# Two channel transforms back to back in the second matrix product of a spectral mixer, with TensorE's order written by hand

## The chip, the cores and the metric

The kernel runs on one core of a Trainium2 chip. The core has a matmul engine (TensorE, PE in the profile), a vector engine (VectorE, DVE), an engine for activations (ScalarE, ACT), GpSimd (POOL) and SyncE (SP), which here only issues DMA. Each engine works through its own queue in order; semaphores make one engine wait for another. PSUM is the memory that matmuls write, in eight banks; SBUF holds everything else.

The metric is the device time of one execution in microseconds. Three runs of the kernel before took 389.78, 391.57 and 392.61 us; their median, 391.57 us, is the time to compare with.

## What is computed

The input x has 2048 tokens (S) and 512 channels (D), in float32. It is normalised over the channels; one branch filters the result in the frequency domain, the other normalises it once more and runs an MLP across the tokens. The two are multiplied and added to x:

```
xn = layernorm(x)
s  = irfft2(rfft2(xn) * (w_r + 1j * w_i))     # over tokens and channels, 2048 x 257 weights
h  = layernorm(xn)
u  = gelu(w1^T h + b1)                                       # over the token axis: 2048 -> 1792
g  = silu(w2^T u + b2)                                       # 1792 -> 2048
y  = x + s * g
```

## The kernel before, in words

The 2048 output rows lie in 16 row blocks of 128. The program has three stages. In the first, each block of x is normalised, the first step of its Fourier transform is taken on TensorE, and part of the product with w1 (GEMM1) is accumulated. In the second, the filter is applied to the spectrum while the rest of GEMM1 runs. The third stage, GEMM2, is the one that the change touches; it takes from about 212 us to the end.

**GEMM2's products.** The row blocks are taken in eight pairs: pair p holds block j0 = p and block j1 = p + 8. A pair is computed by seven half-size products in the manner of Strassen (with Winograd's additions). Each has 21 matmuls (L828): seven blocks of the hidden dimension (the list FORMS) times three, because every float32 operand is split into a high and a low part and three of the four partial products are kept. The seven products of a pair run in the order `ORDER = (1, 2, 5, 6, 3, 7, 4)`. On the hidden side the split operands are made once, and lie in the tiles fd, fa, fb and fc. On the side of w2 they are made for each product: `w2_forms` (L714) loads, adds (L720, L726) and splits, the high part by a copy on ScalarE (L706), the low part by a subtraction on VectorE (L707). The tile w2f has three buffers, so the form of one product is written when the product three places earlier is done.

**PSUM tiles.** Product 1 goes to the tile bx, 2 to by, 5 to bz. Products 6, 7 and 4 are added onto bx and product 3 onto bz. Between two products that share a tile, something must read it: `copied` (L790, ScalarE) takes p1 from bx after product 1, p5 from bz after product 5 and v2 from bx after product 6; `summed` (L798, VectorE) makes c11 after product 2, c12 after product 3, and c22 = bx + p5 after product 7. `gate` (L794, ScalarE) applies the silu, and `finish` (L802, VectorE) multiplies the gate by the spectral result in PSUM bank 0 or 1 and issues the accumulating store.

**The spectral branch inside GEMM2.** For each row block, `gathered` (L756, ScalarE) copies the block's spectrum out of ey into a tile yt. `channels` (L759 to L783) takes the inverse transform over the channels: four matmuls against ci (L763, shown as eight rows in the profile) into PSUM bank 6 (blocks j0) or 7 (blocks j1); od (L765, ScalarE); es (L767, L768), tt (L770, L771) and y (L776 to L779) on VectorE; and the split of y into ch (ScalarE) and cl (VectorE, both L143). The tiles od, es, tt and y have one buffer each. `spectral` (L785) then makes the inverse transform over the tokens with three matmuls of 512 columns (L146 to L148), which need ch and cl, into bank 0 or 1.

In the kernel before, the loop calls `channels` for block j1 behind product 6 and uses it behind product 7. It calls `channels` for the next pair's block j0 behind product 7, and uses it behind product 1 of the next pair.

**What sets the order.** The kernel is written in a layer that schedules: each engine's queue is laid down at build time by a scheduler that takes the instructions by the order of the program and by their readiness. Where a call goes through `keep` (tc.keep_in_program_order), the engine's order is that of the program. The class `Kept` (L124) wraps an engine so that every operation does. TensorE is wrapped so in the second stage; for GEMM2 the line `V, A, T = nc.vector, nc.scalar, nc.tensor` (L685) takes the wrapping off again.

Of the kernel before, what the change touches and what calls it, by code (L numbers as in the profile page):

```python
# [134 lines left out]
def spectral_mixer_kernel(tc, x, w1, b1, w2, b2, wk, we, wx, c_f, c_ft, c_d, c_i, c_g, c_h, out):  # L135
    nc = tc.nc
    V, A, G, T, SY = nc.vector, nc.scalar, nc.gpsimd, nc.tensor, nc.sync
# [4 lines left out]
    def split(hi, lo, src):  # L142
        return A.activation(hi, src, AF.Copy), V.tensor_sub(lo, src, hi.bitcast(F32))  # L143

    def mm3(o, lh, ll, rh, rl, first, last):
        T.matmul(o, lh, rh, start=first, stop=False)  # L146
        T.matmul(o, lh, rl, start=False, stop=False)  # L147
        T.matmul(o, ll, rh, start=False, stop=last)  # L148

    with tc.tile_pool(name="ps", bufs=1, space=PSUM) as psp, ExitStack() as left, ExitStack() as right:  # L150
# [38 lines left out]
        keep = tc.keep_in_program_order  # L189
# [143 lines left out]
        def form_parts(n, i):  # L333
            t, k = form[i][n]
            return t[:, k, :D // 2], t[:, k, D // 2:]
# [155 lines left out]
        T = Kept(T, keep)  # L491
# [193 lines left out]
        V, A, T = nc.vector, nc.scalar, nc.tensor  # L685
        w2p = pool(right, "right", "w2", 3)
        NP, HD = NJ // 2, D // 2
# [66 lines left out]
        def gathered(j):  # L754
            yt = fp.tile([P, 4, P], F32, name=f"yt{j}", tag="yt", bufs=2)
            A.activation(yt.rearrange("p b (l c) -> p b l c", c=2), ey[:, :, :, j], AF.Copy)  # L756
            return yt

        def channels(j, yt):  # L759

            pe = ps[:, 6 + j // NP].rearrange("p (h b c) -> p h b c", b=2, c=P)
            for b in range(4):
                T.matmul(pe[:, b % 2, b // 2], yt[:, b], ci[:, b], start=True, stop=True)  # L763
            od = fp.tile([P, 2, P], F32, name=f"od{j}", tag="od")
            A.activation(od, pe[:, 1], AF.Copy)  # L765
            es = fp.tile([P, 2, 2, P], F32, name=f"es{j}", tag="es")
            V.tensor_add(es[:, 0], pe[:, 0], od)  # L767
            V.tensor_sub(es[:, 1], pe[:, 0], od)  # L768
            t = fp.tile([P, 2, 64], F32, name=f"tt{j}", tag="tt")
            V.tensor_add(t[:, 0], es[:, 1, 1, :64], es[:, 1, 1, 64:])  # L770
            V.tensor_sub(t[:, 1], es[:, 1, 1, 64:], es[:, 1, 1, :64])  # L771
            y = fp.tile([P, D], F32, name=f"y{j}", tag="y")
            yv = y.rearrange("p (s h q c) -> p s h q c", s=2, h=2, c=64)
            ev = es[:, :, 0].rearrange("p h (q c) -> p h q c", c=64)
            ov = es[:, 0, 1].rearrange("p (h c) -> p h c", c=64)
            V.tensor_add(yv[:, 0, :, 0], ev[:, :, 0], ov)  # L776
            V.tensor_sub(yv[:, 1, :, 0], ev[:, :, 0], ov)
            V.scalar_tensor_tensor(yv[:, 0, :, 1], t, RT, ev[:, :, 1], op0=ALU.mult, op1=ALU.add)
            V.scalar_tensor_tensor(yv[:, 1, :, 1], t, -RT, ev[:, :, 1], op0=ALU.mult, op1=ALU.add)  # L779
            ch = fp.tile([P, D], F32R, name=f"ch{j}", tag="ch", bufs=2)  # L780
            cl = fp.tile([P, D], F32R, name=f"cl{j}", tag="cl", bufs=2)
            split(ch, cl, y)
            return ch, cl  # L783

        def spectral(j, y):  # L785
            mm3(ps[:, j // NP], cft[:, 0], cft[:, 1], *y, True, True)

        def copied(name, src):
            t = fp.tile([P, HD], F32, name=name, tag=name.split("_")[0])
            A.activation(t, src, AF.Copy)  # L790
            return t

        def gate(g, j, cols, src, scale):
            A.activation(g[:, cols], src, AF.Silu, bias=b2t[:, j:j + 1], scale=scale)  # L794

        def summed(name, a, b):
            t = fp.tile([P, HD], F32, name=name, tag="c", bufs=2)
            V.tensor_add(t, a, b)  # L798
            return t

        def finish(g, j, cols):
            V.tensor_mul(g[:, cols], ps[:, j // NP, cols], g[:, cols])  # L802
            if j + 1 < NJ:
                G.dma_start(out[:, j, cols], g[:, cols], accum_op=ALU.add)  # L804
            else:
                V.tensor_add(g[:, cols], g[:, cols], xr[:, cols])
                SY.dma_start(out[:, j, cols], g[:, cols])

        left_, right_, whole = slice(0, HD), slice(HD, D), slice(0, D)
        y0 = channels(0, gathered(0))  # L810
        for p in range(NP):
            j0, j1 = p, p + NP
            g0, g1 = (fp.tile([P, D], F32, name=f"g{j}", tag="g", bufs=2) for j in (j0, j1))
            bx, by, bz = ps[:, 2 + p % 2, :HD], ps[:, 4, :HD], ps[:, 5, :HD]
            for k, n in enumerate(ORDER):
                wf = ready.pop(0)
                w = next(wforms, None)
                if w is not None:
                    ready.append(w)
                if k == 1:  # L820
                    yt = gathered(j1)
                if k == 4 and p + 1 < NP:
                    yt = gathered(j0 + 1)
                o = {1: bx, 6: bx, 7: bx, 4: bx, 2: by, 5: bz, 3: bz}[n]
                for m, i in enumerate(FORMS):
                    uh, ul = form_parts(n, i)
                    for a, (wi, ui) in enumerate(((0, uh), (0, ul), (1, uh))):
                        T.matmul(o, wf[:, wi, i], ui, start=m + a == 0 and n in (1, 2, 5), stop=m == NH - 1 and a == 2,  # L828
                                 skip_group_check=n in (6, 3, 7, 4))
                if n == 1:  # L830
                    p1 = copied(f"p1_{p}", bx)
                    spectral(j0, y0)
                elif n == 5:
                    p5 = copied(f"p5_{p}", bz)
                elif n == 2:
                    gate(g0, j0, left_, summed(f"c11_{p}", by, p1), 1.0)
                elif n == 6:
                    v2 = copied(f"v2_{p}", bx)
                    y1 = channels(j1, yt)
                elif n == 3:  # L840
                    gate(g0, j0, right_, summed(f"c12_{p}", bz, v2), 1.0)
                    finish(g0, j0, whole)
                elif n == 7:
                    gate(g1, j1, right_, summed(f"c22_{p}", bx, p5), -1.0)
                    spectral(j1, y1)
                    if p + 1 < NP:
                        y0 = channels(j0 + 1, yt)
                    else:
                        finish(g1, j1, right_)
                else:  # L850
                    gate(g1, j1, left_, bx, -1.0)
                    finish(g1, j1, whole if p + 1 < NP else left_)
# [37 lines left out]
```

## Time and profile before

| What | us |
|---|---|
| median of three runs | 391.57 |
| the profiled execution's own time | 387.47 |
| span of the profile (first to last instruction) | 385.7 |
| mean granted TensorE clock in the profile | 0.993 of full speed |
| TensorE busy with matmuls | 374.0 (97% of the span) |
| VectorE busy | 323.2 (84%) |
| ScalarE busy | 227.6 (59%) |
| GpSimd busy | 78.6 (20%) |

The profile is one execution. The span is what the profile covers, and the execution's own time holds the little that lies around it. In the rows of a timeline the first figure is the start in us from the beginning of the span, the second the length in us; then come the engine, the line of the kernel, the operation, what it writes and reads, the shapes and how many instructions were merged in the row. A bracket gives the idle time of the engine ahead of the row, and what ended it. Rows of a windows view give a stretch, its length, the busy time of TensorE (and of more engines, where asked for) with counts, the granted clock, the share of the DMA engines and GB/s. Matmuls are pipelined and their ends are modelled, so that the distance from one start to the next says more than a row's length.

### The profile page before, as it was taken

Reading aid. Unit: us, or ns where it says so; the run is one execution under the profiler, and the core shown is the slowest. Engines: PE = TensorE matmul, PEld = TensorE weight load, DVE = VectorE, ACT = ScalarE, POOL = GpSimd, SP = SyncE. Lnnn points to the kernel's source line nnn. Section 1 sums busy time; section 2 is a strip of 40 time slices with the busy share of each in tenths; the row PEclk is TensorE's granted clock in tenths of the full one; section 3 lists DMA queues with packets and bytes.
Section 4 is the critical chain, followed back from the end, with each engine's and each line's share of the span. In section 5 each row is a group of like instructions: output and inputs, shape, how many; then the busy total and the mean of one; then the engine's idle time right before and its main releaser. Section 6 shows DMA issues by size and latency. Waiting matters only on the chain.

```text
span 385.7 us, 7939 instructions
## 1 busy us (share of the span) xinstructions
PE 374.0 (97%) x2872; PEld 328.8 (85%) x2872; DVE 323.2 (84%) x734; ACT 227.6 (59%) x412; POOL 78.6 (20%) x133
## 2 busy tenths in 40 slices
PE   7999999999999999999799989999999999999994
PEld 4888888888778878777588979999999999999994
DVE  5899999986579999897995999796979787887873
ACT  4677776764843455575417695565656564646541
POOL 2133233231302333233001003030202020210100
PEclk9999999999999999999899999999999999999999
DMA  8974777312636889988828398896979787885602
GB/s 262 300 251 155 266 254 241 97 55 82 198 77 173 211 226 256 245 226 193 259 71 253 57 274 208 214 215 166 201 153 214 140 230 143 220 165 156 98 0 55
DMA packets 39143, 70.01 MB, mean 182 GB/s; under 512 B 5424, under 2 KB 21440, under 8 KB 38976
## 3 DMA queue, kind: packets, MB, share of 16 engines
q1 hardware_dynamic: 30048, 48.14, 39.8%
q0 software_dynamic: 9056, 21.38, 29.3%
q8 instruction: 22, 0.36, 0.4%
q14 instruction: 17, 0.14, 0.1%
HBM read 61.10 MB, written 8.13 MB: 179 GB/s over the span
## 4 chain that ended last, share of the span: by engine, by line
PE 73%; DVE 9%; DMA 9%; issue 5%; ACT 1%; POOL 1%; SPq 0%; DVEq 0%; POOLq 0%; ACTq 0%
PE ps L828 28%; PE ps L377 20%; PE ps L132 16%; PE ps L241 4%; PE ps L763 3%; DMA s<-in_w_dram 2%; DMA out_dram<-g 2%; DVE w2f L707 2%; DMA w1l<-in_w_dram 2%; PE ps L366 1%; DMA w1s<-in_w_dram 1%; PE ps L147 1%; PE ps L148 1%; DMA hf<-in_c_h_dram 1%; DVE xc L589 1%
## 5 line engine op out<-in xcount | busy, mean ns | idle before, releaser
L377 PE MATMUL ps<-h,w1h 128*128 128x512 f32 x224 | 58.7, 398 | 0.0
L132 PE MATMUL ps<-h,w1h 128*128 128x512 f32 x152 | 49.6, 408 | 0.0
L707 DVE TENSOR_TENSOR w2f<-s,w2f 128x896 fp32r<-128x896 f32 x32 | 34.8, 1092 | 16.6 <-ACT w2f L706 15.8
L377 PEld LDWEIGHTS ps<-h,w1h 128*128 128x128 f32 x224 | 40.9, 188 | 7.9
L828 PE MATMUL ps<-fa,w2f 128*128 128x256 f32 x336 | 43.4, 282 | 0.0
L828 PE MATMUL ps<-fc,w2f 128*128 128x256 f32 x336 | 41.7, 280 | 1.0 <-DVE w2f L707 0.6
L828 PE MATMUL ps<-fb,w2f 128*128 128x256 f32 x336 | 42.5, 281 | 0.1
L828 PEld LDWEIGHTS ps<-fa,w2f 128*128 128x128 f32 x336 | 41.6, 188 | 0.8
L828 PEld LDWEIGHTS ps<-fc,w2f 128*128 128x128 f32 x336 | 40.3, 188 | 1.6 <-DVE w2f L707 0.8
L828 PEld LDWEIGHTS ps<-fb,w2f 128*128 128x128 f32 x336 | 40.4, 188 | 0.5 <-DVE c L798 0.5
L697 POOL DMA_DIRECT2D s<-in_w_dram x16 | 13.9, 870 | 122.0 <-DMA s<-in_w_dram 36.7
L706 ACT ACTIVATE w2f<-s 128x896 fp32r<-128x896 f32 x32 | 30.2, 949 | 14.1 <-DVE s L720 10.9
L132 PEld LDWEIGHTS ps<-h,w1h 128*128 128x128 f32 x152 | 27.7, 192 | 9.9 <-issue 4.9
L707 DVE TENSOR_TENSOR w2f<-a,w2f 128x896 fp32r<-128x896 f32 x24 | 26.0, 1085 | 9.5 <-ACT w2f L706 9.5
L132 PE MATMUL ps<-h,w1l 128*128 128x512 f32 x76 | 30.1, 396 | 2.8 <-DMA w1l<-in_w_dram 2.8
L377 PE MATMUL ps<-h,w1l 128*128 128x512 f32 x112 | 30.6, 389 | 0.0
L706 ACT ACTIVATE w2f<-a 128x896 fp32r<-128x896 f32 x24 | 22.8, 950 | 11.8 <-PE ps L828 7.3
L377 PEld LDWEIGHTS ps<-h,w1l 128*128 128x128 f32 x112 | 21.0, 188 | 4.5
L589 DVE SCALAR_TENSOR_TENSOR xc<-xc,turn,px 128x512 f32<-128x512 f32 x32 | 23.9, 747 | 0.2 <-issue 0.2
L372 DVE TENSOR_TENSOR w1l<-w1r,w1h 128x512 fp32r<-128x512 f32 (+1 forms) x32 | 20.9, 652 | 2.1 <-ACT w1h L369 1.9
L804 POOL DMA_DIRECT2D out_dram<-g x15 | 13.5, 902 | 43.8 <-DVE g L802 43.8
L794 ACT ACTIVATE g<-c,b2t 128x256 f32<-128x256 f32 x24 | 12.1, 505 | 15.9 <-DVE c L798 13.3
(128 smaller groups left out, 765.5 us busy)
## 6 DMA issues: line engine op xcount, KB each, us to landing
a<-in_w_dram SPq DMA_DIRECT2D x24, 448.0 KB, 4.0
wt<-in_wk_dram POOLq DMA_DIRECT2D x16, 512.0 KB, 4.7
s<-in_w_dram SPq DMA_DIRECT2D x16, 448.0 KB, 4.3
s<-in_w_dram POOLq DMA_DIRECT2D x16, 448.0 KB, 6.7
w1s<-in_w_dram SPq DMA_DIRECT2D x36, 128.0 KB, 3.2
w1r<-in_w_dram SPq DMA_DIRECT2D x16, 256.0 KB, 3.6
xc<-px SPq DMA_DIRECT2D x64, 64.0 KB, 4.1
x<-in_x_dram SPq DMA_DIRECT2D x15, 256.0 KB, 3.7
```

The costliest lines, as they stand in the source:

```text
L132: return lambda *args, **kw: self.keep(operation(*args, **kw))
L241: T.matmul(z[:, b], h[:, b * P:(b + 1) * P], c, start=True, stop=True)
L372: keep(V.tensor_sub(dst, src, hi.bitcast(F32)))
L377: T.matmul(ps[:, bank + i], w[wi][:, i * P:(i + 1) * P], hj, start=first and j == 0, stop=last and j == NJ - 1)
L589: V.scalar_tensor_tensor(to, zt, turn[:, k:k + 1], px[:, ::-1], op0=ALU.mult, op1=ALU.add)
L697: G.dma_start(t, w2_half(*added), accum_op=ALU.add)
L706: A.activation(wf[:, 0], v, AF.Copy)
L707: V.tensor_sub(wf[:, 1], v, wf[:, 0].bitcast(F32))
L763: T.matmul(pe[:, b % 2, b // 2], yt[:, b], ci[:, b], start=True, stop=True)
L794: A.activation(g[:, cols], src, AF.Silu, bias=b2t[:, j:j + 1], scale=scale)
L804: G.dma_start(out[:, j, cols], g[:, cols], accum_op=ALU.add)
L828: T.matmul(o, wf[:, wi, i], ui, start=m + a == 0 and n in (1, 2, 5), stop=m == NH - 1 and a == 2, skip_group_check=n in (6, 3, 7, 4))
```

## The change

Three things change in the loop over the pairs, and nothing else:

- both gathers of a pair stand early: block j1's at the second product, as before, and the next pair's block j0 at the third instead of the fifth;
- both calls of `channels` stand behind product 6, one behind the other; `spectral` stays where it was for either block;
- from the second pair on, T is the wrapped TensorE, so that its instructions (those of `channels` and `spectral` too, which use the same T) keep the program's order. In the first pair it is not wrapped.

```diff
--- before.py
+++ after.py
@@ -807,20 +807,20 @@
                 SY.dma_start(out[:, j, cols], g[:, cols])
 
         left_, right_, whole = slice(0, HD), slice(HD, D), slice(0, D)
-        y0 = channels(0, gathered(0))
+        y0 = [channels(0, gathered(0))]
         for p in range(NP):
             j0, j1 = p, p + NP
             g0, g1 = (fp.tile([P, D], F32, name=f"g{j}", tag="g", bufs=2) for j in (j0, j1))
             bx, by, bz = ps[:, 2 + p % 2, :HD], ps[:, 4, :HD], ps[:, 5, :HD]
+            yts = []
+            T = Kept(nc.tensor, keep) if p else nc.tensor
             for k, n in enumerate(ORDER):
                 wf = ready.pop(0)
                 w = next(wforms, None)
                 if w is not None:
                     ready.append(w)
-                if k == 1:
-                    yt = gathered(j1)
-                if k == 4 and p + 1 < NP:
-                    yt = gathered(j0 + 1)
+                if k in (1, 2) and (k == 1 or p + 1 < NP):
+                    yts.append(gathered((j1, j0 + 1)[k - 1]))
                 o = {1: bx, 6: bx, 7: bx, 4: bx, 2: by, 5: bz, 3: bz}[n]
                 for m, i in enumerate(FORMS):
                     uh, ul = form_parts(n, i)
@@ -829,23 +829,21 @@
                                  skip_group_check=n in (6, 3, 7, 4))
                 if n == 1:
                     p1 = copied(f"p1_{p}", bx)
-                    spectral(j0, y0)
+                    spectral(j0, *y0)
                 elif n == 5:
                     p5 = copied(f"p5_{p}", bz)
                 elif n == 2:
                     gate(g0, j0, left_, summed(f"c11_{p}", by, p1), 1.0)
                 elif n == 6:
                     v2 = copied(f"v2_{p}", bx)
-                    y1 = channels(j1, yt)
+                    y1, *y0 = (channels(j, yt) for j, yt in zip((j1, j0 + 1), yts))
                 elif n == 3:
                     gate(g0, j0, right_, summed(f"c12_{p}", bz, v2), 1.0)
                     finish(g0, j0, whole)
                 elif n == 7:
                     gate(g1, j1, right_, summed(f"c22_{p}", bx, p5), -1.0)
                     spectral(j1, y1)
-                    if p + 1 < NP:
-                        y0 = channels(j0 + 1, yt)
-                    else:
+                    if p + 1 == NP:
                         finish(g1, j1, right_)
                 else:
                     gate(g1, j1, left_, bx, -1.0)
```

## The prediction

> **What bounds the kernel now.** The page first, then TensorE's timeline over one pair of row blocks of GEMM2, and the windows row for the same stretch.
>
> ```profile
> span 385.7 us, 7939 instructions
> PE 374.0 (97%) x2872; PEld 328.8 (85%) x2872; DVE 323.2 (84%) x734; ACT 227.6 (59%) x412; POOL 78.6 (20%) x133
> ```
> ```profile
> 278.17 2.54 PE L828 MATMUL ps<-fd,w2f 128*128 128x256 f32 x21
> ...
> 288.67 1.05 PE L763 MATMUL ps<-cd,yt 128*128 128x128 f32 x8
> 289.48 2.72 PE L828 MATMUL ps<-fa,w2f 128*128 128x256 f32 x21
> 292.04 2.63 PE L828 MATMUL ps<-fb,w2f 128*128 128x256 f32 x21
> 294.51 0.39 PE L146 MATMUL ps<-ch,cft 128*128 128x512 f32 x1
> 294.74 0.38 PE L763 MATMUL ps<-cd,yt 128*128 128x128 f32 x2
> ...
> 295.64 0.83 PE L763 MATMUL ps<-cd,yt 128*128 128x128 f32 x6
> 296.23 2.72 PE L828 MATMUL ps<-fb,w2f 128*128 128x256 f32 x21
> 298.79 1.46 PE L828 MATMUL ps<-fd,w2f 128*128 128x256 f32 x11
> ```
> ```profile
> 277.00:299.00 22.00, 22.00 (x183) 21.60 (x183) 18.19 (x39) 12.20 (x22) 3.47 (x4) 1.00 0.84 185
> ```
>
> The timeline shows pair p=3. A pair runs seven products of 21 matmuls in the order 1, 2, 5, 6, 3, 7, 4. Product 1 starts at 278.17, the channel transform of the upper block (8 rows of L763) at 288.67 after product 6, product 3 at 289.48, product 7 at 292.04, the spectral triple (L146 to L148) with the second transform threaded into it at 294.51, product 4 at 296.23, and the next pair at 298.79. The period is 298.79 - 278.17 = **20.62 us**, and the windows row says TensorE is busy in all 22.00 us, VectorE (the third figure) in 18.19. So TensorE sets the pace here with no gap to win, and VectorE has only some 3.8 us of slack in 22: TensorE will wait wherever a needed VectorE instruction stands late in its queue.
>
> The one to look at is c22 (L798), which reads the PSUM tile bx after product 7. Product 4 adds onto the same tile, so its first matmul must wait for c22; in the built program of both kernels it does. VectorE around that point of the same pair, and the ScalarE instructions that feed it:
>
> ```profile
> 291.13 0.42 DVE L767 TENSOR_TENSOR es<-ps,od 128x256 f32<-128x256 f32 x1
> 291.47 0.41 DVE L768 TENSOR_TENSOR es<-ps,od 128x256 f32<-128x256 f32 x1
> 291.92 0.22 DVE L770 TENSOR_TENSOR tt<-es 128x64 f32<-128x64 f32 x1
> ...
> 292.80 0.29 DVE L779 SCALAR_TENSOR_TENSOR y<-tt,es 128x128 f32<-128x128 f32 x1
> 293.00 0.42 DVE L798 TENSOR_TENSOR c<-ps,v 128x256 f32<-128x256 f32 x1
> 293.33 1.09 DVE L707 TENSOR_TENSOR w2f<-a,w2f 128x896 fp32r<-128x896 f32 x1
> 294.33 0.69 DVE L143 TENSOR_TENSOR cl<-y,ch 128x512 fp32r<-128x512 f32 x1
> 294.94 0.69 DVE L802 TENSOR_TENSOR g<-ps,g 128x512 f32<-128x512 f32 x1
> 295.54 0.42 DVE L798 TENSOR_TENSOR c<-ps,p 128x256 f32<-128x256 f32 x1
> ```
> ```profile
> 293.12 0.63 ACT L143 ACTIVATE ch<-y 128x512 fp32r<-128x512 f32 x1
> 293.66 0.49 ACT L794 ACTIVATE g<-c,b2t 128x256 f32<-128x256 f32 x1
> ```
>
> c22 ends at 295.54 + 0.42 = 295.96, and product 4 starts at 296.23: the wait is covered by 0.27 us, and only because the second transform lies in between. In the last pair there is no second transform, and the wait shows:
>
> ```profile
> 377.61 0.40 PE L148 MATMUL ps<-ch,cft 128*128 128x512 f32 x1
> 378.10 2.74 PE L828 MATMUL ps<-fb,w2f 128*128 128x256 f32 x21
> ```
> ```profile
> 377.63 0.41 DVE L798 TENSOR_TENSOR c<-ps,p 128x256 f32<-128x256 f32 x1
> ```
>
> The spectral triple issues every 0.23 us (294.51 to 294.74), so product 4 could have started at 377.84; c22 ended at 378.04 and product 4 started at 378.10, 0.06 later. That is the price of one wake-up.
>
> **The change part by part.**
>
> *TensorE's work.* No instruction is added or removed. The second transform moves from the spectral triple to right behind the first. Both together take 2 x (289.48 - 288.67) = 1.62. Product 3 takes 292.04 - 289.48 = 2.56 behind a transform, product 7 294.51 - 292.04 = 2.47: switching back from a transform costs 0.09. From 288.67 product 4 can then start after 1.62 + 2.56 + 2.47 + 3 x 0.23 = 7.34, against 296.23 - 288.67 = 7.56 now. **Gain 0.22 us a pair**, at 296.01, if nothing waits.
>
> *VectorE's queue.* The diff moves `channels(j0 + 1, ...)` ahead of product 3, and the built program shows where its vector instructions land from p=1 on: es, tt, y of the upper block; es of the next block; cl of the upper block; tt and y of the next; c12; the L707 of the next pair's form 1; cl of the next; the g product L802; **only then c22**. In the kernel before, the next block's chain stood behind c22. What is newly in front, by start-to-start steps: es 2 x 0.34 (291.13 to 291.47) = 0.68; tt and y 293.00 - 291.92 = 1.08; cl 294.94 - 294.33 = 0.61; in all 2.37. One more wait: the upper block's ch ends at 293.12 + 0.63 = 293.75, while VectorE, done with the next es at 293.00 + 0.68, wants it at 293.68: 0.10 with the wake-up. c22 then runs from 295.54 + 2.47 = 298.01 to 298.43, and product 4 starts at 298.49. ScalarE doesn't add to it: c12 would start at 295.47 and end at 295.89, the next ch (0.63) and the gate (0.49) end by 296.7, and cl and L802 want them at 296.8 and 297.4.
>
> **The stall is 298.49 - 296.01 = 2.48 us a pair.** Queued behind the waiting matmul is all of TensorE: product 4, the next products 1, 2, 5, 6. Nothing gives it back. VectorE's chain starts anew from the end of product 6, through the ScalarE copy of form 4 into a buffer that product 6 frees, and so shifts along. New period 20.62 - 0.22 + 2.48 = **22.88**. I looked for a second wait: after c22 VectorE does form 2, then waits for the left gate, which waits for product 4 (301.0 + 0.49 for the gate), then L802, L707 of form 5, L720 (taken as L707's 1.09, same shape), a ScalarE copy, L707 of form 6, done near 307; product 6 starts at 309.1. Some 2 us spare, so none.
>
> *The order written by hand.* From p=1 on TensorE's built order differs between the two kernels only in the moved transform, so keeping it costs nothing by itself. Between the first pair and the second it does:
>
> ```profile
> 233.00 0.40 PE L146 MATMUL ps<-ch,cft 128*128 128x512 f32 x1
> 233.24 0.63 PE L828 MATMUL ps<-fd,w2f 128*128 128x256 f32 x4
> ...
> 234.77 2.63 PE L828 MATMUL ps<-fb,w2f 128*128 128x256 f32 x21
> ```
> ```profile
> 231.49 0.42 DVE L798 TENSOR_TENSOR c<-ps,v 128x256 f32<-128x256 f32 x1
> ...
> 234.07 0.41 DVE L798 TENSOR_TENSOR c<-ps,p 128x256 f32<-128x256 f32 x1
> ```
> ```profile
> 231.73 0.62 ACT L143 ACTIVATE ch<-y 128x512 fp32r<-128x512 f32 x1
> ```
>
> Before, the scheduler filled the wait for c22 (ends 234.48) with matmuls of the next pair's product 1 (fd). That filler is gone, and c22 moves back as well: c12 at 231.49, one es to 232.16, cl when ch is there (231.73 + 0.62 and a wake-up) 232.38 to 232.98, the other es to 233.32, L802 (0.60) to 233.92, tt and y to 235.00, L707 (1.00) to 236.00, cl to 236.61, c22 to 237.02. Product 4 starts at 237.08; the triple is done at 233.00 + 0.69 = 233.69. **Stall 3.39.**
>
> *One wait goes.* In the second pair L147 waited for cl:
>
> ```profile
> 253.84 0.50 PE L147 MATMUL ps<-cl,cft 128*128 128x512 f32 x1 [0.38 <-DVE cl L143]
> ```
>
> That 0.38 lies ahead of the new stall and vanishes. cl of the upper block now ends near 294.4, well ahead of the triple at 295.3.
>
> *DMA queues.* SP's and POOL's order of issues is unchanged in the built program, and a longer period gives every load more time: nothing counted.
>
> Sum without the clock: 3.39 + 6 x (2.48 - 0.22) - 0.38 = **+16.6 us** (pairs p=1 to 6; the last pair keeps its own wait).
>
> *The granted clock.* A stall that long may cost more than itself. Windows of 3.41 us, TensorE's busy time, then the granted clock:
>
> ```profile
> 182.65:186.06 3.41, 2.23 (x10) 1.00 0.86 252
> 186.06:189.47 3.41, 1.84 (x34) 1.00 1.13 312
> 189.47:192.88 3.41, 3.41 (x54) 0.50 0.66 181
> 220.19:223.60 3.41, 2.50 (x20) 1.00 0.68 220
> ```
>
> After a window with 1.57 us idle the clock was halved for one whole window, a loss of 3.41 x 0.5 = **1.7 us**; after windows with 1.18 and 0.91 idle it wasn't. If windows lie on a fixed grid and x us of idle in one brings a fall, a stall of 2.48 that lands anywhere brings it in (3.41 - 2.48 + 2 x (2.48 - x)) / 3.41 of cases: 81% at x = 1.57, 27% at x = 2.48. The row's matmuls have modelled ends (0.39 long, issued every 0.23), so the true x lies above 1.57; I take the middle, 54%: three of six, and the 3.39 stall as a fourth. 4 x 1.7 = **+6.8**, bounds 0 and 7 x 1.7 = 11.9.
>
> [...]
>
> **Total.** +16.6 + 6.8 = +23.4: the profiled execution of 387.47 (span 385.7) would become 410.9. It lies 4.1 below the median of the three runs, 391.57 (389.78 to 392.61); on that median the forecast is **415.0 us**.
>
> **The rivals.**
>
> [...]
> 2. *A fall at each stall:* 408.2 + 11.9 = 420.1.
> 3. *Half the stall.* If VectorE gains on the walk, by a shorter queue ahead of the upper es, c22 comes about 1.2 us earlier in each pair: 408.2 - 7 x 1.2 = 400. Against: that es waits for form 4's copy after product 6, which doesn't move.
> 4. *Not slower: c22 stays covered.* It decides at one point: no more than 0.05 us may be added ahead of c22 (296.01 - 295.96). Then only the switches and the 0.38 go: -(6 x 0.22) - 0.38 = -1.7, 389.9. For it: VectorE is idle some 3.8 us in 22. Against: that idle time lies elsewhere in the pair, and the built queue puts 2.37 us in front.
>
> **How the numbers follow.** Forecast (stalls with two to six falls) 0.52, rival 1 0.30, rival 2 0.06, rival 3 0.07, rival 4 0.05. The range reaches from rival 1 with stalls a quarter shorter (408.2 - 4.2 = 404) to rival 2 (420). A measurement of this kernel tells about 1% from no change; only rival 4 lies within that: slower 0.95, within 1% 0.04, faster 0.01.
>
> **What the changed profile would show.** Product 4's first matmul with an idle time of about 2.5 us ahead of it, released by VectorE's L798, in pairs 1 to 6 and about 3.4 in the first; VectorE's L767 of the next block ahead of c12; 16 rows of L763 in one piece; a period of 22.9, or 24.6 where the clock fell; a granted clock of 0.5 for 3.4 us behind some stalls. It is wrong if c22 ends within 0.7 us of product 7, or if another instruction than c22 releases product 4.

## The result, and the profile after

The changed kernel takes **415.58 us** (median of 6 runs, 411.37 to 417.43) against 391.59 for the kernel before (6 runs, 389.46 to 392.61): a ratio of **1.0614**, with a 95% interval of 1.0576 to 1.0652. It is 24.0 us slower. The forecast was 415.0, in a range of 404 to 420.

The page of the changed kernel, whose profiled execution took 416.76 us: the span, then the engines' busy time.

```profile
span 415.0 us, 7945 instructions
PE 384.1 (93%) x2872; PEld 336.1 (81%) x2872; DVE 323.3 (78%) x734; ACT 226.5 (55%) x412; POOL 78.4 (19%) x133
```

VectorE does the same work as before (323.3 against 323.2 us). TensorE has the same 2872 matmuls, yet is busy 10 us longer, and 31 us of the span are idle instead of 12. What it waited for (total us, times, longest us):

```profile
PE ps L132 <- DVE c L798: 13.8, 6, 2.3
PE ps L132 <- DMA w1l<-in_w_dram: 5.0, 1, 5.0
PE ps L828 <- DVE c L798: 3.2, 1, 3.2
```

The first and the third row are one wait in seven pairs: product 4 waits for L798. (From the second pair on, every matmul shows L132, the line in `Kept`.) The DMA wait lies ahead of GEMM2, where the two kernels have the same code; before, it was

```profile
PE ps L132 <- DMA w1l<-in_w_dram: 2.8, 2, 2.6
```

It varies between executions (3.6 to 5.3 in seven of the experiments below), and with it the start of GEMM2. The spans differ by 29.3 us, but 5.3 of that has passed before GEMM2 starts. So lengths of GEMM2 are compared here, from the first matmul of product 1 to the last product 4: **165.90 us before** (212.20 to 378.10), **189.86 after** (217.54 to 407.40). That is +23.96, near the difference of the medians (23.99). It is the difference of two single executions all the same, and those of the changed kernel differ: their mean granted clock goes from 0.982 in the shortest (411.37 us) down to 0.966, and is 0.969 in the profiled one, so the number of stretches at a halved clock isn't the same in each.

TensorE's timeline of the changed kernel: product 4 of all seven pairs that wait, each with the product 1 behind it, and pair p=3 from its transforms on (the first figure is the start, the second the length; in brackets the idle time ahead and what ended it):

```profile
238.61 0.40 PE L148 MATMUL ps<-ch,cft 128*128 128x512 f32 x1
242.21 4.27 PE L828 MATMUL ps<-fb,w2f 128*128 128x256 f32 x21 [3.20 <-DVE c L798]
246.32 2.63 PE L132 MATMUL ps<-fd,w2f 128*128 128x256 f32 x21
...
266.80 2.75 PE L132 MATMUL ps<-fb,w2f 128*128 128x256 f32 x21 [2.31 <-DVE c L798]
269.38 2.63 PE L132 MATMUL ps<-fd,w2f 128*128 128x256 f32 x21
...
289.86 4.27 PE L132 MATMUL ps<-fb,w2f 128*128 128x256 f32 x21 [2.31 <-DVE c L798]
293.98 2.63 PE L132 MATMUL ps<-fd,w2f 128*128 128x256 f32 x21
...
304.29 1.95 PE L132 MATMUL ps<-cd,yt 128*128 128x128 f32 x16
...
311.49 0.39 PE L132 MATMUL ps<-ch,cft 128*128 128x512 f32 x1
314.18 4.22 PE L132 MATMUL ps<-fb,w2f 128*128 128x256 f32 x21 [2.30 <-DVE c L798]
318.24 2.63 PE L132 MATMUL ps<-fd,w2f 128*128 128x256 f32 x21
...
338.45 2.74 PE L132 MATMUL ps<-fb,w2f 128*128 128x256 f32 x21 [2.31 <-DVE c L798]
341.02 2.63 PE L132 MATMUL ps<-fd,w2f 128*128 128x256 f32 x21
...
361.50 4.27 PE L132 MATMUL ps<-fb,w2f 128*128 128x256 f32 x21 [2.31 <-DVE c L798]
365.61 2.64 PE L132 MATMUL ps<-fd,w2f 128*128 128x256 f32 x21
...
386.06 4.12 PE L132 MATMUL ps<-fb,w2f 128*128 128x256 f32 x21 [2.28 <-DVE c L798]
390.02 2.63 PE L132 MATMUL ps<-fd,w2f 128*128 128x256 f32 x21
```

Both transforms now stand in one piece (the x16 at 304.29, ahead of product 3). The spectral triple issues its last matmul at 311.49, so product 4 could follow 0.23 later, at 311.72; it starts at 314.18. **Counted this way, as in the prediction, the stall is 2.46 us**; the bracket says 2.30, since it counts from the modelled end of that last matmul. In the same way the first pair's stall is 242.21 - 238.84 = 3.37 (its triple ends with a matmul issued at 238.61).

The length of product 4 comes in two sizes: about 2.75 in pairs p=1 and p=4, and 4.1 to 4.3 in the other five. There the granted clock fell to 0.50 for 3.41 us (windows rows of two such stretches follow further down). The periods, from product 1 to product 1, follow: 23.06 and 22.78 in the two pairs without a fall, 24.60, 24.26, 24.59 and 24.41 in p=2, 3, 5 and 6.

VectorE's timeline in pair p=3, the queue ahead of c22:

```profile
308.83 0.42 DVE L767 TENSOR_TENSOR es<-ps,od 128x256 f32<-128x256 f32 x1
...
309.50 0.68 DVE L143 TENSOR_TENSOR cl<-y,ch 128x512 fp32r<-128x512 f32 x1
...
311.18 0.41 DVE L798 TENSOR_TENSOR c<-ps,v 128x256 f32<-128x256 f32 x1
311.52 1.08 DVE L707 TENSOR_TENSOR w2f<-a,w2f 128x896 fp32r<-128x896 f32 x1
312.52 0.68 DVE L143 TENSOR_TENSOR cl<-y,ch 128x512 fp32r<-128x512 f32 x1
313.12 0.68 DVE L802 TENSOR_TENSOR g<-ps,g 128x512 f32<-128x512 f32 x1
313.72 0.41 DVE L798 TENSOR_TENSOR c<-ps,p 128x256 f32<-128x256 f32 x1
```

c12 is the L798 at 311.18, c22 the last row. It ends at 314.13, and product 4 starts 0.05 later. The next block's es, tt, y and cl (308.83, the rows left out, which are its other es, tt and y, and the cl at 312.52; the cl at 309.50 is the upper block's own) stand ahead of it.

### The profile page after: what moved, and what is told of

The parts are those of the page before. It is cut to its first block, busy times and chain, and to the rows that moved or that the text cites. A ratio compares the mean times of both kernels' runs of the same rounds, so it can differ in the third digit from the quotient of the medians.

```text
span 415.0 us, 7945 instructions
## 1 busy us (share of the span) xinstructions
PE 384.1 (93%) x2872; PEld 336.1 (81%) x2872; DVE 323.3 (78%) x734; ACT 226.5 (55%) x412; POOL 78.4 (19%) x133
## 4 chain that ended last, share of the span: by engine, by line
PE 73%; DVE 11%; issue 6%; DMA 4%; ACT 3%; SPq 2%; POOL 1%; DVEq 0%; POOLq 0%
PE ps L132 47%; PE ps L377 18%; PE ps L241 3%; DVE cl L143 2%; DMA w1l<-in_w_dram 2%; DVE w2f L707 2%; PE ps L366 1%; DMA gf<-in_c_g_dram 1%; PE ps L828 1%; ACT w2f L706 1%; DVE c L798 1%; SPq L344 1%; DVE es L767 1%; DMA xc<-px 1%; SPq L572 1%
## 5 line engine op out<-in xcount | busy, mean ns | idle before, releaser
L132 PE MATMUL ps<-fb,w2f 128*128 128x256 f32 x294 | 43.5, 310 | 13.9 <-DVE c L798 13.8
L132 PEld LDWEIGHTS ps<-fb,w2f 128*128 128x128 f32 x294 | 41.4, 217 | 16.9 <-DVE c L798 16.9
L132 PE MATMUL ps<-h,w1h 128*128 128x512 f32 x152 | 50.0, 411 | 0.0
L706 ACT ACTIVATE w2f<-s 128x896 fp32r<-128x896 f32 x32 | 30.2, 948 | 22.9 <-DVE s L726 16.6
L132 PE MATMUL ps<-fa,w2f 128*128 128x256 f32 x294 | 37.3, 281 | 0.0
L132 PEld LDWEIGHTS ps<-fa,w2f 128*128 128x128 f32 x294 | 35.9, 188 | 0.6
L132 PEld LDWEIGHTS ps<-h,w1h 128*128 128x128 f32 x152 | 28.0, 194 | 9.9 <-issue 4.9
L132 PE MATMUL ps<-fc,w2f 128*128 128x256 f32 x294 | 35.4, 278 | 0.0
L132 PE MATMUL ps<-h,w1l 128*128 128x512 f32 x76 | 30.5, 402 | 5.0 <-DMA w1l<-in_w_dram 5.0
L132 PEld LDWEIGHTS ps<-fc,w2f 128*128 128x128 f32 x294 | 34.7, 188 | 0.0
L802 DVE TENSOR_TENSOR g<-ps,g 128x512 f32<-128x512 f32 (+1 forms) x17 | 11.1, 654 | 26.2 <-ACT g L794 26.2
```

What stands on the lines that cost most here:

```text
L132: return lambda *args, **kw: self.keep(operation(*args, **kw))
L706: A.activation(wf[:, 0], v, AF.Copy)
```

## The experiments

The theory has two parts. First: c22 is late on VectorE because the next block's chain stands ahead of it, and TensorE's fixed order leaves nothing to do meanwhile. Second: stalls of this length bring falls of the granted clock. A fall is a stretch in which the granted clock is 0.50 (3.41 us long in each of the five pairs above). The rivals: one of the edits costs the time by itself (the fixed order, or the transforms' new place), or the stalls come without falls.

### Each edit alone

**order_alone** is the kernel before with the one line that keeps TensorE's order:

```diff
+            T = Kept(nc.tensor, keep) if p else nc.tensor
```

> TensorE keeps the program's order from the second pair on, and the transforms stay where they were in the kernel before. Theory (product 4 waits for a late c22, and neither edit does it alone): c22 stands where it stood, so the only new waits are about 0.5 us at product 4 of the first pair, whose filler is gone, and 0.1 to 0.3 us at L147 of each later pair, since no transform is threaded into the triple: 391.6 + 1.2 = 392.8 us, clock as before. Rival (the program's order by itself costs, because TensorE can't go on with the next pair): most of the 24 us, 407 us or more.

Measured: 391.56 us (10 runs), ratio 1.0043 (1.0010 to 1.0075); GEMM2 167.78 us. Product 4 waits for c22 in one pair alone, by 0.2 us; in six pairs the triple waits 0.17 us for cl. The period is 20.95 us, against 20.62 before.

**adjacent_alone** is the changed kernel without that line.

> The transforms stand back to back as in the changed kernel, TensorE's order is left to the scheduler in all pairs. Theory: VectorE's queue has c22 as late as in the changed kernel, but the built program puts 12 matmuls of the next pair's product 1 ahead of product 4, so that TensorE has 12 x 0.118 = 1.4 us of work in the wait, and product 7 ends later as well: 391.6 + 0.6 = 392.2 us, no fall of the clock in GEMM2, no wait above 0.5 us. Rival (putting both transforms ahead of product 3 costs by itself, on TensorE or as work on VectorE): 405 us or more.

Measured: 392.44 us (10 runs), ratio 1.0045 (1.0016 to 1.0073); GEMM2 167.49 us. TensorE's timeline of adjacent_alone around product 4 of one pair, then VectorE's c22:

```profile
299.39 0.41 PE L827 MATMUL ps<-fd,w2f 128*128 128x256 f32 x2
299.63 0.83 PE L763 MATMUL ps<-cd,yt 128*128 128x128 f32 x6
300.74 1.80 PE L827 MATMUL ps<-fd,w2f 128*128 128x256 f32 x13 [0.28 <-DVE w2f L707]
302.38 2.64 PE L827 MATMUL ps<-fb,w2f 128*128 128x256 f32 x21
```
```profile
301.81 0.41 DVE L798 TENSOR_TENSOR c<-ps,p 128x256 f32<-128x256 f32 x1
```

Here c22 ends at 302.22, 2.83 us after product 4 could have followed the triple (299.39): later than in the changed kernel (314.13 - 311.72 = 2.41). But the scheduler, free to choose, puts six of the transform's rows and 15 of the 21 matmuls of the next pair's product 1 (fd) into the wait, and it costs 0.28.

So **neither edit alone costs more than half a per cent; the two together cost 6.1%**. The moved transforms make c22 late, and the kept order forbids the work that would fill the wait. Both rivals of one edit fall.

### Take the cause away

**c22_ahead** keeps both edits, and takes the next block's chain out of c22's way: `channels` is cut into its matmuls and the rest, and the rest of the next block is called, and kept, behind c22. The g product of the first block (L802, `finish`) moves behind c22 as well; the lines that keep VectorE's order and those that cut `channels` in two aren't shown.

```diff
-                    y1, *y0 = (channels(j, yt) for j, yt in zip((j1, j0 + 1), yts))
+                    pes = [channels_mm(j, yt) for j, yt in zip((j1, j0 + 1), yts)]
+                    y1 = channels_rest(j1, pes[0])
...
                     gate(g1, j1, right_, summed(f"c22_{p}", bx, p5), -1.0)
+                    finish(g0, j0, whole)
                     spectral(j1, y1)
-                    if p + 1 == NP:
+                    if p + 1 < NP:
+                        y0 = channels_rest(j0 + 1, pes[1])
+                    else:
```

> TensorE's order and both transforms as in the changed kernel; the vector part of the next block's transform, the g product L802 of the first block and c22 are recorded in such an order, and kept so on VectorE, that c22 stands ahead of both. Theory: product 4 doesn't wait above 0.3 us; cl of the next block is later, so L147 of the next pair waits about 0.6 us: 391.6 + 3.7 = 395 us, no fall of the clock in GEMM2. Rival (the order or the place of the matmuls is the cause): 410 us or more. If c22 is the cause but VectorE is simply too full, the wait appears elsewhere at its old size: 405 us or more.

Measured: 397.28 us (4 runs), ratio 1.0178 (1.0106 to 1.0250); GEMM2 171.34 us. The wait on c22 is gone from the list, and the clock doesn't fall in GEMM2. What is left is a smaller wait, behind product 1 (TensorE's timeline of c22_ahead, the triple of one pair):

```profile
264.37 0.39 PE L132 MATMUL ps<-ch,cft 128*128 128x512 f32 x1
265.20 0.51 PE L132 MATMUL ps<-cl,cft 128*128 128x512 f32 x1 [0.44 <-DVE cl L143]
```

The second matmul of the triple comes 0.83 after the first instead of 0.23: 0.60 us a pair, because the next block's cl is now the one that comes late. The period is 21.3 us, against 20.62 before. Taking c22's wait away therefore returns 18.5 of the 24.0 us of GEMM2 (the falls of the clock that went with it included), and moves a part of the lateness to another matmul. The time came out some 2 us above what was expected.

**c22_by_copy** leaves VectorE's queue as it is, and frees the PSUM tile another way: ScalarE copies bx behind product 7, and c22 reads the copy.

```diff
-                    gate(g1, j1, right_, summed(f"c22_{p}", bx, p5), -1.0)
+                    gate(g1, j1, right_, summed(f"c22_{p}", copied(f"v7_{p}", bx), p5), -1.0)
```

> The changed kernel, but c22 is made from a copy of the tile that ScalarE takes behind product 7, so that product 4 waits for that copy and not for VectorE; VectorE's queue is as late as in the changed kernel. Theory: the copy stands behind the gate that needs c12, about 0.9 us after the triple; product 4 waits 0.9 us in pairs 2 to 7, released by ScalarE's L790, too short for the clock to fall: 391.0 + 3.4 = 394.5 us. Rival (VectorE is too full with both transforms ahead of product 7, whatever product 4 waits for): other waits take its place, 405 us or more.

Measured: 395.77 us (4 runs), ratio 1.0122 (1.0084 to 1.0160); GEMM2 170.66 us, no fall of the clock in it. TensorE's waits of c22_by_copy, then VectorE's c22 of one pair and TensorE's product 4 of the same pair:

```profile
PE ps L132 <- ACT v L790: 4.9, 6, 1.1
```
```profile
303.49 0.42 DVE L798 TENSOR_TENSOR c<-v,p 128x256 f32<-128x256 f32 x1
```
```profile
302.43 2.74 PE L132 MATMUL ps<-fb,w2f 128*128 128x256 f32 x21 [0.77 <-ACT v L790]
```

Product 4 starts 1.06 us before c22 does. It waits for the copy alone, 0.8 us a pair in the mean; the time is 1.3 us above what was expected. The price was thus not the late c22, but that c22 was the reader that product 4 had to wait for.

### The clock: fill the wait, and leave it as it is

**wait_filled** puts 16 matmuls that nothing reads (into an unused part of a PSUM bank; they add nothing to the result) behind the triple. The wait for c22 stays as long, but TensorE is busy in it.

```diff
                     spectral(j1, y1)
+                    if p + 1 < NP:
+                        for _ in range(FILL):
+                            T.matmul(ps[:, 4, HD:], cft[:, 0], cft.rearrange("p a b -> p (a b)"), start=True, stop=True)
```

> The changed kernel, with 16 matmuls of 256 columns, which add nothing to the result, between the spectral triple and product 4 of each pair but the last; they write a half of a PSUM bank that nothing reads. c22 stays late. Theory: TensorE is busy through 1.9 of the 2.3 us, product 4 starts when it did, and the granted clock doesn't fall in pairs 2 to 7: 415.6 less five falls of 1.7 = 407 us (405 to 409). Rival 1 (the falls don't come from the idle time): they stay, 415 us. Rival 2 (a fall costs nothing, since VectorE is the bound in that stretch): the clock stays at 1.0 and the time at 415 us.

Measured: 409.58 us (4 runs), ratio 1.0487 (1.0424 to 1.0549); GEMM2 184.26 us. TensorE's waits of wait_filled (one line further down than in the changed kernel):

```profile
PE ps L829 <- DVE c L799: 2.9, 1, 2.9
PE ps L133 <- DVE c L799: 2.3, 6, 0.4
```

In the six later pairs 0.4 us of idle time is left and the clock stays whole. In the first, where the order isn't kept, the scheduler left only three of the fillers in the wait; 2.9 us stay idle, and there the clock falls. Four falls fewer and the stalls as long: GEMM2 is 5.6 us shorter, **1.4 us a fall**. The time lies just above the 405 to 409 that were expected: the first pair's fall stayed, and a fall is worth less than the 1.7 us put down for it.

**filled_5** and **filled_2** are the same with 5 and 2 fillers, so that 1.7 and 2.1 us stay idle in each wait from the second pair on (3.1 in the first, where the scheduler puts the fillers elsewhere).

> As wait_filled, with 5 matmuls instead of 16 in each wait; they add nothing to the result. In the changed kernel's trace the clock fell after windows of the 3.41 us grid with 1.97 us or more idle and did not fall after windows with 1.80 and 1.82. Theory (a window falls when about 1.9 us of it are idle): 5 x 0.119 = 0.6 us leave 1.7 us idle, below that mark wherever the grid lies, so the clock falls behind none of the stalls of pairs 2 to 7, only behind the first pair's (3 us): as wait_filled, 409 to 410 us. Rival (each idle stretch adds to the chance, however short): one to three falls in pairs 2 to 7.

> As wait_filled, with 2 matmuls in each wait: 2.07 us stay idle. Theory: the clock falls behind those stalls of which 1.9 us lie in one window of the grid, (3.41 - 2.07 + 2 x 0.17) / 3.41 = 49% of the places, about three of six, and the first pair's: 409.6 + 3 x 1.65 = 414.5 us (411 to 417); and each fall or its absence agrees with the idle share of its window, read from the trace. [...]

Measured, one execution each: 410.94 and 413.27 us; GEMM2 185.35 and 187.83. With 1.7 us idle none of the six later pairs falls; with 2.1 three of six do. filled_5 took 0.9 us more than the 410 expected, since the first pair's fall lasted two windows there; in filled_2 the first pair has none. The windows of filled_2 (start and end, length, TensorE's busy time, the granted clock, DMA share, GB/s), cut on the grid on which its falls begin:

```profile
236.48:239.89 3.41, 1.65 (x12) 1.00 0.78 293
239.89:243.31 3.42, 2.07 (x18) 1.00 0.73 116
...
284.27:287.68 3.41, 1.34 (x9) 1.00 1.06 207
287.68:291.10 3.42, 3.42 (x19) 0.50 0.66 85
308.16:311.57 3.41, 1.55 (x11) 1.00 1.06 209
311.57:314.98 3.41, 3.19 (x27) 1.00 0.89 133
355.94:359.36 3.42, 1.47 (x10) 1.00 1.07 220
359.36:362.77 3.41, 3.29 (x15) 0.50 0.86 126
```

The first pair's gap of 3.11 us lies across the first two windows, 1.76 and 1.35 idle, and no fall follows. The gap of 2.07 us at 285.12 lies whole in one window, and the clock falls in the next. Between 1.86 idle (308.16, no fall) and 1.95 (355.94, a fall) lies the threshold in these rows. A grid with the same step of 3.41 us fits the changed kernel: a gap of the same length brings a fall or none by where it lies.

```profile
262.87:266.28 3.41, 1.62 (x11) 1.00 1.04 218
266.28:269.70 3.42, 2.90 (x24) 1.00 0.87 133
286.77:290.18 3.41, 1.10 (x6) 1.00 1.06 208
290.18:293.59 3.41, 3.41 (x18) 0.50 0.75 103
...
334.55:337.96 3.41, 1.59 (x11) 1.00 0.97 178
...
382.34:385.75 3.41, 1.44 (x10) 1.00 0.66 120
385.75:389.16 3.41, 3.10 (x14) 0.50 0.55 69
```

1.79 us idle in pair p=1, 2.31 in p=2 and 1.97 in p=6: no fall, a fall, a fall. In p=4 (the row at 334.55), whose gap of 2.31 is cut in the same way as that of p=1, 1.82 lie in one window, and the clock stays whole.

### A version without either cost

**c22_ahead_free** is c22_ahead without the line that keeps TensorE's order: transforms together, c22 ahead, scheduler free.

> As c22_ahead, with TensorE's order left to the scheduler in all pairs. Theory: the next pair's product 1 takes up the waits for cl that c22_ahead had (0.44 us a pair), and the transforms stay in one piece, so that the switches saved show: 391.0 + 0 to 2, at best -0.4; no version of this schedule can win more than about 1.5 us, since TensorE is busy all through GEMM2. Rival (a schedule with both transforms together is better once c22 is out of the way): 388 us or less.

Measured: 392.48 us (7 runs), ratio 1.0054 (1.0030 to 1.0079); GEMM2 167.92 us. It has almost no waits left in the later pairs, and is still not faster than before: TensorE is the bound there, busy in 142.95 of the 143 us from 235 to 378, and has nothing to win but the switches between transforms and products. Of its 2.0 us over the kernel before, 0.9 is one wait of the first pair, for VectorE's fc (L302), which the kernel before doesn't have in its trace; the later periods are 20.8 us instead of 20.62. No version that was run beats the kernel before.

## Why the prediction was right

- **The stall.** Predicted 2.48 us a pair and 3.39 in the first, from a walk along VectorE's queue; measured 2.46 and 3.37 by the same count. Releaser (L798), place (product 4), the order on VectorE and the two transforms in one piece are those of the prediction. Two small misses cancel in it: from the start of the transforms product 4 could follow after 7.43 us (304.29 to 311.72) and not 7.34, so that the gain was 0.13 and not 0.22, and c22 ended 9.84 us after that start and not 9.76. c22_ahead and c22_by_copy show the cause: with c22 out of the way, or not the reader, the wait is gone.
- **The sum without the clock.** Predicted +16.6. Measured: +23.96 in GEMM2 less what the falls cost. A halved window slows product 4 alone here. From its start to that of the next product 1 it takes 4.11, 4.12, 4.06, 4.11 and 3.96 us in the five pairs with a fall, against 2.58 and 2.57 in p=1 and p=4: 7.5 us in all, 1.5 a fall, which leaves +16.5. The period without a fall was predicted as 22.88 (measured 23.06 and 22.78), with one as 24.6 (24.26 to 24.60).
- **The falls.** Predicted four at 1.7 us; the profiled execution had five at 1.5: 7.5 us instead of 6.8. The 1.7 takes half of the window for lost. But matmuls of 256 columns start every 0.213 us in the halved window at 290.18 and every 0.118 us at full clock, so that the 16 of that window lose 16 x 0.095 = 1.5; at 385.75, where TensorE is busy in only 3.10 us of the window, the fall costs 1.4. One fall more and a lower price for each nearly cancel, and the number of falls differs between executions, so it is in part luck that 415.0 and 415.58 lie so close together. wait_filled shows that the falls belong to the idle time and not to the change: with the stalls kept and filled, they go. Rival 1, stalls without falls, gave 408.2 (the median of 391.57 and the sum of 16.6), and falls by this; so does rival 2, a fall at each stall, by pairs p=1 and p=4. No run shows the 408.2, on which the range and rivals 2 and 3 are built too: wait_filled, with one fall left in GEMM2, took 409.58.
- **The threshold.** The prediction took the middle between 1.57 and 2.48, by which 54% of the stalls fall. The row it had, 1.57 idle with a fall behind it, looks at odds with 1.86 idle without one. Counted by issue rather than by modelled ends, four matmuls at 0.23 and 0.47 of small ones make 1.39 busy, 2.02 idle, in that window, and the two windows that bound the threshold, whose gaps begin 0.16 earlier by that count, have 2.02 and 2.11. This brings them together within what the trace resolves. By this count 1.39 us of that window were busy, less than half of its 3.41; by the modelled ends it was 1.84, more than half. The middle that the prediction took, 2.03, is close to the threshold by issue. The length of a gap alone doesn't tell a fall: in filled_2 the gap of 2.07 us at 285.12 brought a fall, the one of 3.11 us in the first pair none. Nor did one of 3.57 us ahead of GEMM2 in c22_ahead_free (185.29 to 188.86): an edge of that trace's grid, at 187.15 (59 steps of 3.413 us ahead of its one fall, at 388.54), cuts it into 1.86 and 1.71.
- **Rival 3** (half the stall, 400) and **rival 4** (c22 stays covered, 389.9) fall by the stall's measured size.
- **Incomplete in one step.** The prediction said that keeping the order "costs nothing by itself" from p=1 on, and gave it a price only between the first and the second pair. order_alone bears out the sentence but for 0.33 us a pair (20.95 against 20.62), of which 0.17 is the wait for cl; adjacent_alone shows what it leaves out: the kept order is the second condition of every stall. Without it the same late c22 costs 0.5%. The sum was right since both edits were in the kernel; whoever had taken the prediction for a price of the moved transforms alone would have been wrong by some 22 us (392.44 against 415.0).

## What to carry to other kernels

Ahead of moving work that feeds an in-order engine, find the reader of each PSUM tile that the next product adds to, and walk that engine's queue up to it: here 2.37 us more ahead of one vector instruction became 2.46 us on TensorE. Fixing an engine's order takes away the filler that hides another engine's lateness, so price the two together and run each alone (here 6.1% together, 0.43% and 0.45% alone). Where gaps can't be avoided, the runs speak for keeping the idle time in any 3.41-us window below about 1.8 us: in GEMM2 no fall followed a window with up to 1.86, and only one fall seen here followed a full-speed window with less (1.57 by the profile's count, in the kernel before). A few matmuls that nothing reads keep it below that mark, if the gap can't be filled with work: with five of them, in filled_5, 1.7 us stayed idle and none of the six later pairs fell.

## What the runs showed of the hardware

- The falls begin on a fixed grid. In the changed kernel those of GEMM2 begin at 242.39, 290.18, 314.07, 361.86 and 385.75: 14, 7, 14 and 7 steps of 3.413 us apart, and each lasts one such step at a granted clock of 0.50. The place of the grid differs between executions (a fall begins at 242.39 here, at 240.18 in filled_5).
- The falls go not with the length of a gap but with the idle time inside one window of that grid: in GEMM2 no fall followed a window with up to 1.86 us idle by the profile's count (filled_2, 308.16), and one followed each with 1.95 or more (filled_2, 355.94). So 1.95 of 3.41 us, 57% of a window, was enough, with TensorE busy in the other 1.47.
- A halved window that is itself partly idle can be followed by a second one. In filled_5 the first pair's gap reached 0.79 us into the halved window at 240.18, and the next stayed at half; after a halved window with 0.31 us idle (385.75 in the changed kernel) the clock came back at once. These few cases don't place the boundary more closely than between 0.31 and 0.79.

```profile
236.77:240.18 3.41, 1.08 (x7) 1.00 0.75 283
240.18:243.59 3.41, 2.62 (x12) 0.50 0.93 151
243.59:247.01 3.42, 3.42 (x18) 0.50 1.03 183
```
